# Loading one piece of the output weight in two transfers, 108 and 20 partitions, in a decode block on one core

## The chip, the cores and the metric

The kernel runs on one core of one Trainium2 chip. The metric is the device time of one launch in microseconds (us). The kernel before takes 1302.96 us, the median of three runs (1302.74 to 1303.16).

## The reference

The block normalises its input and adds three things: the input, an attention block over a cache of 4096 keys, and a small MLP. Everything is float32.

```python
x = A_x                                   # [4, 1, 512]
xn = layernorm(x)
q = (xn @ A_wq).reshape(4, 1, 32, 128)    # 32 heads of 128
scores = einsum("bhqd,bhkd->bhqk", q, A_k_cache) * 128**-0.5    # caches: [4, 32, 4096, 128]
o = einsum("bhqk,bhkd->bhqd", softmax(scores), A_v_cache)
att = o.reshape(4, 1, 4096) @ A_wo        # A_wo: [4096, 512]
# mlp: sequence length is 1, so the token shift leaves only zeros and x1 = xn
mlp = xn + gelu(layernorm(xn) @ B_w3) @ B_w4
return x + att + mlp                      # [4, 1, 512]
```

The two caches are 268 MB each. All the weights together are about 24 MB.

## The kernel before, in words

The 128 pairs of batch and head are handled in 32 steps of four heads (`NJ = 32`, `G = 4`). A step reads 8 MB of keys into one of two buffers (`ks[0]`, `ks[1]`) and 8 MB of values into `vs`. VectorE (DVE) multiplies the keys by the query (L329) and sums (L330), in two halves. ScalarE (ACT) takes the exponential (L348). TensorE (PE) multiplies the probabilities with the values (L382).

All these loads are issued by SyncE (SP), one after the other in the order of the code, on one DMA queue (q1 in the profile). SP waits for a semaphore before most issues: `summed` says that DVE has used half a key buffer, `done` says that a step's values have been used.

After the last step comes the tail, where this change lies. The output weight `wo` is laid out as 128 partitions of 32 rows (`wo_r`, partition p holds rows 32p to 32p + 31, each of 512 floats or 2 KB), and it goes into the key buffer of the last step. SP issues it as soon as DVE has read that buffer for the last time (`SUMMED[LAST]`), in seven pieces that become smaller:

```python
wo_cuts = ((0, 16), (16, 24), (24, 28), (28, 30), (30, WC - 1))
```

These are rows per partition: the five pieces hold 16, 8, 4, 2 and 1 rows per partition, and two more pieces hold the halves of row 31 (L292). Each piece has its own semaphore (`wo0` to `wo6`), and each of its partitions is one contiguous run in memory: 32, 16, 8, 4, 2, 1 and 1 KB. "The piece with two rows per partition" is the fourth, `wo3`: 128 runs of 4 KB, 512 KB in all.

PE waits for the pieces one by one and multiplies the attention output `X` with each row. Rows 0 to 23 go into `y` (L419). Rows 24 to 30 go into `total` through the helper `blocks4` (L151), and so does the sum over `y`, which ACT has copied to `os` first (L425). The two halves of row 31 come last (L434). Then DVE (L436) and ACT (L437) copy the result out of PSUM, and two small DMAs store it (L441).

Of the kernel before, what the change touches and what calls it, by code (L numbers as in the profile page):

```python
# [44 lines left out]
P = 128  # L45
# [4 lines left out]
PE, DVE, ACT = mybir.EngineType.PE, mybir.EngineType.DVE, mybir.EngineType.Activation  # L50
# [38 lines left out]
def decode_block(ctx: ExitStack, tc: tile.TileContext, x, k, v, wq, wo, w3, w4, out):  # L89
    nc = tc.nc  # L90
# [10 lines left out]
    FT = F // 4  # L101
    WC = H * DH // P
    LAST = NJ - 1

    def sb(name, *shape):
        return nc.alloc_sbuf_tensor(name, [P, *shape], F32).ap()
# [37 lines left out]
    def rows(flat, j):  # L144
        n = G * S * DH
        return flat[j * n:(j + 1) * n].rearrange("(p n) -> p n", p=P)

    def blocks4(start, stop, w, m, src):

        for t in range(4):  # L150
            i = nc.tensor.matmul(total[32 * t:32 * t + m, :], w, src[:, P * t:P * t + P], start=start, stop=stop)  # L151
        return i

    do = Steps(nc)
    wo_sems = [nc.alloc_semaphore(f"wo{n}") for n in range(7)]
    sems = {n: nc.alloc_semaphore(n) for n in (
        "x", "w3", "wq", "k0", "k1", "landed", "last", "w4", "go", "pv", "copied", "poz",
        "half0", "half1", "nm", "dve", "summed", "expd", "done", "bye", "out")}
    wo_sb = ks[LAST % 2].rearrange("p (c n) -> p c n", c=WC)
    wo_cuts = ((0, 16), (16, 24), (24, 28), (28, 30), (30, WC - 1))  # L160
# [3 lines left out]
    def load(o, i, sem, by, *after, queue="SP"):  # L164
        return do(queue, lambda e: e.dma_start(o, i), *after, done=(sems[sem], 16, by))
# [22 lines left out]
        out=ident, in_=ident, compare_op=ALU.not_equal, fill=1.0, base=0, pattern=[[-1, P]],  # L188
# [64 lines left out]
    for c in range(NC):  # L253
        for t in range(4):
# [23 lines left out]
             for i, n in enumerate((0, HALF))]  # L278
    for j in range(LAST - 1):
        if j > 0:  # L280
            load(ks[j % 2], rows(kf, j + 2), f"k{j % 2}", None, SUMMED[j])
        load(vs, rows(vf, j + 1), "landed", None, DONE[j])
    last_in = load(ks[(LAST - 1) % 2], rows(vf, LAST), "last", 16, SUMMED[LAST - 1])
    w4_in = load(w4_sb, w4.rearrange("(p m) n -> p m n", m=NF), "w4", 16, DONE[LAST - 1])
    do.wait("SP", [SUMMED[LAST]])
    wo_r = wo.rearrange("(p c) n -> p c n", c=WC)
    for (c0, c1), sem in zip(wo_cuts, wo_sems):
        nc.sync.dma_start(wo_sb[:, c0:c1], wo_r[:, c0:c1]).then_inc(sem, 16)
    half = D // 2
    for n, sem in enumerate(wo_sems[-2:]):  # L290
        n *= half
# [10 lines left out]
    nc.gpsimd.sem_inc(sems["k0"], 16)  # L302
    d = do("POOL", lambda e: e.memset(g4, 0.0), DONE[LAST - 1])
    g4_ok = do("POOL", lambda e: e.tensor_copy(g4[:, :, 0:B], gT[:, 0:4, :]), d, gT_ok)
# [4 lines left out]
    with nc.Fori(0, NJ // 2, engines=OrderedEngineSet([DVE]), head_slot={DVE: 192}) as j:  # L309
        e, n = nc.vector, 0  # L310
# [92 lines left out]
    for m in range(NF):  # L403
        t, g, n = (m, g4[:, m, :], 32) if m < 4 else (m % 4, gT[:, m, :], B)
# [7 lines left out]
    ys = os.rearrange("p m d -> p (m d)")  # L412
    do.wait("PE", [X_ok])
    for (c0, c1), sem in zip(wo_cuts, wo_sems):
        do.wait("PE", [(sem, 16)])
        for c in range(c0, c1):
            if c < 24:
                t = (c + 2) % 4
                i = nc.tensor.matmul(y[32 * t:32 * t + B, :], X[:, c, :], wo_sb[:, c], start=False, stop=(c >= 20))  # L419
            else:  # L420
                i = blocks4(False, False, X[:, c, :], B, wo_sb[:, c])
        d = do("PE", lambda e: i)

        if c1 == 24:
            ys_ok = do("ACT", lambda e: e.copy(ys, y), d)  # L425
        elif c1 == 28:
            do.wait("PE", [ys_ok])
            blocks4(False, False, sel, 32, ys)
# [15 lines left out]
    nc.sync.sem_inc(sems["bye"], 1)  # L444
    nc.scalar.sem_inc(sems["bye"], 1)
    nc.gpsimd.wait_ge(sems["bye"], 2)
    nc.clear_and_free_semaphores([*do.sem.values(), *wo_sems, *(h for n, h in sems.items() if n != "out")])
    do.wait("SP", [stored])
    nc.sync.sem_inc(sems["out"], -32)

# [27 lines left out]
```

## Time and profile before

| what | value |
|---|---|
| median of three runs | 1302.96 us |
| the profiled execution, from its first to its last instruction (its span) | 1301.5 us |
| what the median has beyond that span | 1.46 us |
| busy share of DVE, PE, ACT | 89%, 28%, 7% |
| DMA: bytes read, mean rate over the span | 561 MB, 431 GB/s |
| issue of the first piece of `wo` | 1267.41 us |
| first matmul with `wo` | 1289.46 us |
| first matmuls with the two halves of row 31 (their weight loads) | 1299.12 and 1299.44 us |

No other time is recorded for the profiled execution than its span; the runs were made without a profile. Differences within the trace are used as they stand, and a sum is made against the span and carried over to the median. In the windows, "DMA share" is the busy share of the core's 16 DMA engines, so a share times 16 is the number of engines at work. "PEld" is a weight load of PE, which shows when PE got past a wait. Times in the timeline are from the start of the span.

### The profile page before, as it was taken

Reading aid. Unit: us, or ns where it says so; the run is one execution under the profiler, and the core shown is the slowest. Engines: PE = TensorE matmul, PEld = TensorE weight load, DVE = VectorE, ACT = ScalarE, POOL = GpSimd, SP = SyncE. Lnnn points to the kernel's source line nnn. Section 1 sums busy time; section 2 is a strip of 40 time slices with the busy share of each in tenths; the row PEclk is TensorE's granted clock in tenths of the full one; section 3 lists DMA queues with packets and bytes.
Section 4 is the critical chain, followed back from the end, with each engine's and each line's share of the span. In section 5 each row is a group of like instructions: output and inputs, shape, how many; then the busy total and the mean of one; then the engine's idle time right before and its main releaser. Section 6 shows DMA issues by size and latency. Waiting matters only on the chain. (4 is left out here: it accounts for less than half of the span.)

```text
span 1301.5 us, 6687 instructions
## 1 busy us (share of the span) xinstructions
PE 368.7 (28%) x2652; PEld 132.8 (10%) x2652; DVE 1164.4 (89%) x323; ACT 93.5 (7%) x332; POOL 2.5 (0%) x14
## 2 busy tenths in 40 slices
PE   4121332321233321133331133332123332123337
PEld 2000111100011100011110011110011110001112
DVE  2599999999999999999999999999999999999990
ACT  0100000000000000000000000000000000000001
POOL 0000000000000000000000000000000000000000
PEclk9555666655666655666655566665566665566668
DMA  9999999999999999999999999999999999999998
GB/s 404 448 421 449 423 441 427 435 435 425 443 423 447 423 447 421 441 429 431 439 421 447 423 447 423 445 423 437 433 425 445 421 447 423 447 423 443 425 426 367
DMA packets 10830, 561.08 MB, mean 431 GB/s; under 512 B 1212, under 2 KB 1476, under 8 KB 1736
## 3 DMA queue, kind: packets, MB, share of 16 engines
q1 hardware_dynamic: 10808, 561.00, 99.7%
q8 instruction: 3, 0.05, 0.0%
q14 instruction: 3, 0.02, 0.0%
q10 hardware_dynamic: 16, 0.01, 0.0%
HBM read 561.00 MB, written 0.01 MB: 431 GB/s over the span
## 5 line engine op out<-in xcount | busy, mean ns | idle before, releaser
L329 DVE TENSOR_TENSOR ks<-ks,qb 128x8192 f32<-128x8192 f32 x64 | 556.3, 8692 | 63.7 <-DVEq L297 58.7
L330 DVE TENSOR_REDUCE sc<-ks 128x64 f32<-128x8192 f32 x64 | 555.9, 8686 | 2.2
L382 PE MATMUL pv<-vs,pw 128*32 128x512 f32 x1984 | 286.9, 743 | 874.9 <-PEq L297 874.9
L382 PEld LDWEIGHTS pv<-vs,pw 128*32 128x32 f32 x1984 | 79.2, 133 | 1057.9 <-issue 1057.9
L353 ACT COPY os<-pv 128x512 f32<-128x512 f32 x32 | 18.7, 585 | 827.8 <-ACTq L297 827.8
L348 ACT ACTIVATE pw<-sc,small 32x128 f32<-32x128 f32 x128 | 50.9, 398 | 278.1 <-ACTq L297 276.9
L387 PE MATMUL poz<-sel,os 128*128 128x4 f32 x256 | 32.8, 252 | 28.0 <-PEq L297 28.0
L387 PEld LDWEIGHTS poz<-sel,os 128*128 128x128 f32 x256 | 31.0, 191 | 56.1 <-issue 56.1
L348 ACT ACTIVATION_READ_ACCUMULATOR pw<-sc,small 32x1 f32 x128 | 23.5, 184 | 0.0
L436 DVE COPY os<-total 4x128 f32<-4x128 f32 x2 | 0.6, 282 | 16.2 <-PE total L434 16.2
L335 DVE TENSOR_REDUCE small<-sc 128x1 f32<-128x128 f32 x32 | 9.2, 286 | 4.7
L363 DVE RECIPROCAL rz<-oz 128x96 f32<-128x96 f32 (+1 forms) x2 | 1.1, 552 | 12.6 <-ACT oz L355 12.5
L389 PE MATMUL poz<-rs,ones 128*128 128x4 f32 x64 | 11.7, 253 | 0.0
L245 DVE STREAM_TRANSPOSE vs<-pw 128x1024 f32<-128x1024 f32 x1 | 1.2, 1245 | 10.9 <-ACT pw L244 10.9
L321 DVE STREAM_TRANSPOSE qb<-qg 128x128 f32<-128x128 f32 x32 | 10.0, 312 | 1.1
L202 DVE TENSOR_REDUCE lns<-vs 4x1 f32<-4x512 f32 x1 | 0.7, 674 | 11.3 <-DMA vs<-in_A_x_dram 11.3
L320 DVE COPY qg<-qT 128x4 f32 x32 | 5.4, 170 | 4.9 <-issue 4.9
L389 PEld LDWEIGHTS poz<-rs,ones 128*128 128x128 f32 x64 | 9.7, 192 | 0.0
L215 PE MATMUL pt<-vs,pw 4*128 4x4 f32 x16 | 4.0, 372 | 18.1 <-DVE pw L209 18.1
L419 PE MATMUL y<-ks,X 128*4 128x512 f32 x48 | 8.0, 835 | 3.5 <-DMA ks<-in_A_wo_dram 3.5
L355 ACT COPY oz<-poz 128x8 f32 x32 | 5.3, 165 | 50.8 <-ACTq L297 50.8
L382 PE MATMUL pv<-ks,pw 128*32 128x512 f32 x64 | 8.5, 692 | 0.0
(75 smaller groups left out, 74.8 us busy)
## 6 DMA issues: line engine op xcount, KB each, us to landing
ks<-in_A_k_cache_dram SPq DMA_DIRECT2D x2, 4096.0 KB, 26.9
vs<-in_B_w_dram SPq DMA_DIRECT2D x2, 3584.0 KB, 23.1
ks<-in_A_wo_dram SPq DMA_DIRECT2D x1, 4096.0 KB, 21.9
ks<-in_A_wo_dram SPq DMA_DIRECT2D x1, 2048.0 KB, 26.5
ks<-in_A_wo_dram SPq DMA_DIRECT2D x1, 1024.0 KB, 28.6
ks<-in_A_wo_dram SPq DMA_DIRECT2D x1, 512.0 KB, 29.4
ks<-in_A_k_cache_dram SPq DMA_DIRECT2D x31, 42.2
vs<-in_A_v_cache_dram SPq DMA_DIRECT2D x31, 26.8
```

Source lines behind the costliest of these rows:

```text
L320: step(e.tensor_copy(qg, pairs[:, s, bass.ds(j, 1)].rearrange("p o n -> p (o n)")))
L321: step(e.transpose(qb.rearrange("p (n m) -> p n m", m=HP), qg.unsqueeze(2).to_broadcast([P, DH // HP, HP])))
L329: step(e.tensor_tensor(out=kt, in0=kt, in1=qb.unsqueeze(1).to_broadcast([P, w, DH]), op=ALU.mult))
L330: step(e.reduce_sum(sc[s][:, c:c + w], kt, axis=AX.X))
L335: step(e.reduce_max(rm, sc[s], axis=AX.X))
L348: i = nc.scalar.activation(pw[hp, :, 4 * h:4 * h + 4], sc[s][hp, :].rearrange("p (g w) -> p g w", w=4), AF.Exp, bias=small[hp, s, 1:2], sc ...
L353: nc.scalar.copy(os, pv.rearrange("p (m d) -> p m d", m=4)).then_inc(sems["copied"], 1)
L355: nc.scalar.copy(ozs[:, s, :, bass.ds(j, 1)].rearrange("p n o h -> p n (o h)"), poz[:, 0:2 * G].rearrange("p (n h) -> p n h", n=2)).then_i ...
L382: i = nc.tensor.matmul(pv[32 * t:32 * t + 32, :], pw[:, g, :], vt[:, 4 * g:4 * g + 4, :], start=(g < 4), stop=(g >= NG - 4))
L387: nc.tensor.matmul(poz[:, 0:G], os[:, m, :], sel.rearrange("p (h m) -> p m h", m=4)[:, m, 0:G], start=(m == 0), stop=(m == 3))
L389: nc.tensor.matmul(poz[:, G:2 * G], ones.to_broadcast([P, P]), rs, start=True, stop=True).then_inc(sems["poz"], 1)
L419: i = nc.tensor.matmul(y[32 * t:32 * t + B, :], X[:, c, :], wo_sb[:, c], start=False, stop=(c >= 20))
```

## The change

The fourth piece, `wo3`, is no longer one transfer. Its partitions 0 to 107 are loaded where the whole piece was, between `wo2` and `wo4`. Its partitions 108 to 127 are loaded by a transfer of their own, which SP issues directly behind the first piece `wo0`, with its own semaphore `low`. PE waits for both semaphores before it uses rows 28 and 29.

```diff
+    FEW, TOP = 3, 108
...
+    low_sem = nc.alloc_semaphore("low")
...
-    for (c0, c1), sem in zip(wo_cuts, wo_sems):
-        nc.sync.dma_start(wo_sb[:, c0:c1], wo_r[:, c0:c1]).then_inc(sem, 16)
+    for n, ((c0, c1), sem) in enumerate(zip(wo_cuts, wo_sems)):
+        top = TOP if n == FEW else P
+        nc.sync.dma_start(wo_sb[:top, c0:c1], wo_r[:top, c0:c1]).then_inc(sem, 16)
+        if n == 0:
+            c0, c1 = wo_cuts[FEW]
+            nc.sync.dma_start(wo_sb[TOP:, c0:c1], wo_r[TOP:, c0:c1]).then_inc(low_sem, 16)
...
     for (c0, c1), sem in zip(wo_cuts, wo_sems):
-        do.wait("PE", [(sem, 16)])
+        do.wait("PE", [(sem, 16), *([(low_sem, 16)] if (c0, c1) == wo_cuts[FEW] else [])])
```

The order in which SP issues its last transfers, before. A row gives the line, the tile and its source, and partitions by elements per partition (1024 elements are the two rows of `wo3`):

```order
L165 DMA vs<-in_B_w_dram 128x7168 [waits done]
L288 DMA ks<-in_A_wo_dram 128x8192 [waits summed]
L288 DMA ks<-in_A_wo_dram 128x4096
L288 DMA ks<-in_A_wo_dram 128x2048
L288 DMA ks<-in_A_wo_dram 128x1024
L288 DMA ks<-in_A_wo_dram 128x512
L292 DMA ks<-in_A_wo_dram 128x256 x2
L441 DMA out_dram<-os 4x256 [waits nACT,nDVE]
```

The same place on SP now:

```order
L167 DMA vs<-in_B_w_dram 128x7168 [waits done]
L291 DMA ks<-in_A_wo_dram 128x8192 [waits summed]
L294 DMA ks<-in_A_wo_dram 20x1024
L291 DMA ks<-in_A_wo_dram 128x4096
L291 DMA ks<-in_A_wo_dram 128x2048
L291 DMA ks<-in_A_wo_dram 108x1024
L291 DMA ks<-in_A_wo_dram 128x512
L298 DMA ks<-in_A_wo_dram 128x256 x2
L447 DMA out_dram<-os 4x256 [waits nACT,nDVE]
```

The transfer of 20 partitions is new in second place; the fourth piece keeps its place with 108 partitions, and six issues move back by one.

On PE, the end of the program before, from the last wait for a four-row piece on, with the semaphores that each group waits for:

```order
L151 MATMUL total<-ks,X 4x128 [waits wo2]
L151 MATMUL total<-ks,X 4x128 x15
L151 MATMUL total<-os,sel 32x128 [waits nACT]
L151 MATMUL total<-os,sel 32x128 x3
L151 MATMUL total<-ks,X 4x128 [waits wo3]
L151 MATMUL total<-ks,X 4x128 x7
L151 MATMUL total<-ks,X 4x128 [waits wo4]
L151 MATMUL total<-ks,X 4x128 x3
L434 MATMUL total<-ks,X 4x128 [waits wo5]
L434 MATMUL total<-ks,X 4x128
L434 MATMUL total<-ks,X 4x128 [waits wo6]
L434 MATMUL total<-ks,X 4x128
```

And now:

```order
L152 MATMUL total<-ks,X 4x128 [waits wo2]
L152 MATMUL total<-ks,X 4x128 x15
L152 MATMUL total<-os,sel 32x128 [waits nACT]
L152 MATMUL total<-os,sel 32x128 x3
L152 MATMUL total<-ks,X 4x128 [waits low,wo3]
L152 MATMUL total<-ks,X 4x128 x7
L152 MATMUL total<-ks,X 4x128 [waits wo4]
L152 MATMUL total<-ks,X 4x128 x3
L440 MATMUL total<-ks,X 4x128 [waits wo5]
L440 MATMUL total<-ks,X 4x128
L440 MATMUL total<-ks,X 4x128 [waits wo6]
L440 MATMUL total<-ks,X 4x128
```

No matmul moves; the group for rows 28 and 29 has one wait more. DVE, ACT and GpSimd keep their instructions in their order.

More of the change, by code (lines that the diff above doesn't have):

```diff
@@ L446, in decode_block @@
     nc.gpsimd.wait_ge(sems["bye"], 2)
-    nc.clear_and_free_semaphores([*do.sem.values(), *wo_sems, *(h for n, h in sems.items() if n != "out")])
+    nc.clear_and_free_semaphores([*do.sem.values(), *wo_sems, low_sem, *(h for n, h in sems.items() if n != "out")])
     do.wait("SP", [stored])
```

## The prediction

> **What bounds the kernel now.** I read the page's DMA queues first, then the table of windows, then the timeline of the tail. The page says that one queue keeps the engines busy for all of the span:
>
> ```profile
> q1 hardware_dynamic: 10808, 561.00, 99.7%
> ```
>
> So the time up to the tail is the time of 561 MB, and the change touches neither those bytes nor their order until the first piece of `wo`. What it can change is the tail. Its windows (columns: stretch in us, its length, then busy time and count of PE, PEld, DVE, ACT, POOL, then PE clock, DMA share, GB/s):
>
> ```profile
> 50.00:1250.00 1200.00, 314.57 (x2220) 112.32 (x2220) 1129.95 (x282) 83.23 (x308) 0.00 (x0) 0.61 1.00 434
> ...
> 1297.00:1297.50 0.50, 0.50 (x19) 0.21 (x10) 0.00 (x0) 0.00 (x0) 0.00 (x0) 1.00 0.71 248
> 1297.50:1298.00 0.50, 0.50 (x28) 0.46 (x20) 0.00 (x0) 0.48 (x1) 0.00 (x0) 1.00 0.30 111
> 1298.00:1298.50 0.50, 0.50 (x24) 0.37 (x20) 0.00 (x0) 0.11 (x1) 0.00 (x0) 1.00 0.21 74
> 1298.50:1299.00 0.50, 0.50 (x28) 0.39 (x18) 0.00 (x0) 0.00 (x0) 0.00 (x0) 1.00 0.14 47
> ```
>
> Two things stand here. At a share of 1.00 the 16 engines move 434 GB/s, so one engine moves 27.1 GB/s and a run of 4 KB costs it 4096 / 27.1 = 0.151 us. And the engines do not finish together: 0.71 x 16 is 11.4 engines at work, then 4.8, 3.4 and 2.2. About eleven are done by 1297.5, while two or three go on for almost 1.5 us. If three engines last to the end, 2.2 of 3 times 0.5 us puts them at 1298.87. The other 0.4 engine of the window before is then a fourth that ends near 1298.2, and a fifth ends near 1297.9.
>
> Why some are late can be seen in the same queue table, taken for three short stretches (32.8 to 33.2, 1273 to 1274.6 and 1293 to 1293.5; columns: packets, MB, share of 16 engines' time):
>
> ```profile
> q8 instruction: 1, 0.02, 15.6%
> ...
> q8 instruction: 1, 0.02, 4.3%
> q14 instruction: 1, 0.01, 1.2%
> ...
> q8 instruction: 1, 0.02, 13.6%
> ```
>
> Instructions are fetched by the same engines. The three q8 packets held one engine for 0.156 x 0.4 x 16 = 1.0 us, 0.043 x 1.6 x 16 = 1.1 us and 0.136 x 0.5 x 16 = 1.1 us. That is the size of the lag of the late ones. Since all engines otherwise run at one pace without a pause, an engine that is once behind stays behind.
>
> Now what the late engines cost. The timeline of the tail (weight loads, then matmuls, then ACT; the brackets hold the idle time before and what ended it):
>
> ```profile
> 1295.13 0.10 PEld L419 LDWEIGHTS y<-ks,X 128*4 128x4 f32 x4 [0.44 <-issue]
> ...
> 1296.88 0.10 PEld L151 LDWEIGHTS total<-ks,X 128*4 128x4 f32 x4 [0.37 <-DMA ks<-in_A_wo_dram]
> ...
> 1298.16 0.16 PEld L151 LDWEIGHTS total<-os,sel 128*32 128x32 f32 x8
> 1298.30 0.65 PEld L151 LDWEIGHTS total<-ks,X 128*4 128x4 f32 x24
> 1299.12 0.10 PEld L434 LDWEIGHTS total<-ks,X 128*4 128x4 f32 x4 [0.17 <-DMA ks<-in_A_wo_dram]
> 1299.44 0.10 PEld L434 LDWEIGHTS total<-ks,X 128*4 128x4 f32 x4 [0.22 <-DMA ks<-in_A_wo_dram]
> ...
> 1289.46 7.99 PE L419 MATMUL y<-ks,X 128*4 128x512 f32 x48 [3.48 <-DMA ks<-in_A_wo_dram]
> 1297.27 1.05 PE L151 MATMUL total<-ks,X 128*4 128x128 f32 x32
> ...
> 1297.52 0.58 ACT L425 COPY os<-y 128x512 f32<-128x512 f32 x1 [11.13 <-PE y L419]
> ```
>
> PE starts on the first piece at 1289.46 and has no gap until the two halves of row 31. There it waits for a DMA twice, 0.17 and 0.22 us. These 0.39 us are all that an earlier end of the late engines can bring. The rest of PE's tail hangs on its own matmuls and on ACT's copy. In the other direction nothing covers: a later end of the last engine goes straight into the 0.22 us wait and the time.
>
> **The change, part by part.**
>
> How the rows fall on the engines. The packets show how a transfer is split. First a stretch of 4.5 us with the load of `x` (4 partitions, the q10 row), then the last 39.5 us:
>
> ```profile
> DMA packets 40, 2.11 MB, mean 468 GB/s; under 512 B 4, under 2 KB 4, under 8 KB 8
> ...
> q10 hardware_dynamic: 8, 0.01, 0.5%
> ...
> DMA packets 1223, 14.47 MB, mean 366 GB/s; under 512 B 152, under 2 KB 416, under 8 KB 672
> ```
>
> The load of 4 rows has 8 packets: 4 rows and 4 tiny ones that close it. In the last stretch there are 152 tiny ones: 8 for the two stores of 4 rows, and 144 = 9 x 16 for the nine transfers of 128 rows that end in it. So each engine that takes part closes its share once; 128 rows go to 16 engines, 8 rows each, and 4 rows to 4 engines, one each. Both are equal shares. If shares must be equal, 108 rows can go to no more than 12 engines (9 rows each) and 20 rows to no more than 10 (2 each), as 16 to 13 do not divide 108 and 16 to 11 do not divide 20. No row shows either of these sizes, so this is taken from the two that are shown.
>
> With those shares, four engines lose all 8 of their rows of `wo3`: 8 x 0.151 = 1.21 us less. Twelve get one row more, 0.15 us, and ten of the sixteen get two rows from the new transfer, 0.30 us. An engine that has both carries 3 rows more, 0.45 us. The trace does not number the engines, so it doesn't say which kind the late ones are.
>
> [...]
>
> The end of the last engine. The bounds are -0.39 us (both waits gone) and +0.45 us (a late engine carries three rows more). If the three late ones are among the four that lose rows, they end at 1298.87 - 1.21 = 1297.7, and the fourth becomes the last: 1298.2 + 0.45 = 1298.65, that is 0.22 us earlier than now. I take -0.22 us, inside the -0.39 us. It is a guess a little over even: the late engines, three by the windows, are no more than the four that are relieved, while a single one left out turns the sign.
>
> The order of issue. SP spends 0.50 us on each issue:
>
> ```profile
> 1267.41 2.50 SPq L288 DMA_DIRECT2D ks<-in_A_wo_dram  x5
> 1269.96 0.90 SPq L292 DMA_DIRECT2D ks<-in_A_wo_dram  x2
> ...
> ks<-in_A_wo_dram SPq DMA_DIRECT2D x1, 4096.0 KB, 21.9
> ks<-in_A_wo_dram SPq DMA_DIRECT2D x1, 2048.0 KB, 26.5
> ks<-in_A_wo_dram SPq DMA_DIRECT2D x1, 1024.0 KB, 28.6
> ```
>
> One more issue in second place moves the other six back by 0.50 us. The DMA queue is over 20 us behind the issues (21.9 us from the issue of the first piece to its landing), so this costs nothing. Without that backlog it would be 0.50 us. SP has nothing after them but the store, 29 us later.
>
> Two rows more ahead of the second and third piece: 0.30 us on ten engines. The second piece lands about 1267.9 + 26.5 = 1294.4, and PE takes row 16 (the 33rd weight load of L419) at 1295.13. 0.7 us cover the 0.30. The third piece is awaited until 1296.88, but the matmuls behind that weight load start at 1297.27, when PE is free. 0.39 us cover 0.30; if they didn't, ACT's copy up to 1298.10 is late next, and it hangs on `y` alone. I take 0, at most 0.1 us.
>
> PE's added wait for `low`. These rows land right behind the first piece, near 1289.5, and PE asks at 1298.30. Queued behind it are the matmuls of rows 28 to 31. The nearest row is the wait for `wo3` in the same place, where the weight loads of 1298.16 and 1298.30 follow each other without a gap. I take 0, at most 0.1 us for one more instruction.
>
> The sum is -0.22 us on the span of 1301.5, and on the median 1302.96 - 0.22 = 1302.7 us. The median has 1.46 us that lie outside the span, which the change doesn't touch.
>
> **The rivals.** Differences under 0.2% (2.6 us) can't be told from no change in this kernel; all but one of these cases lie within.
>
> *A late engine is loaded, not relieved.* One of the three late ones is among the ten that carry three rows more: the last half of row 31 comes 0.45 us later, 1303.4 us. For it: twelve engines get more and only four less, and one late engine among them decides. Against it: only that all three share the cause of their lag, and may share their place. [...]
>
> *The change does not do what it says.* The transfers of 108 and 20 rows are spread as evenly as 128 were, 8 rows per engine in sum, or a late engine gains and loses about as much. Then only the order of rows differs, and the time stays 1303.0 us. The 4-row transfer with one row on each of 4 engines neither excludes nor supports it.
>
> *The split falls on far fewer engines.* If the number must divide 16 as well, as both sizes that the trace shows (16 and 4) do, 108 rows go to 4 engines, 27 each, and 20 to 4, 5 each. Four engines would carry 32 rows where they carried 8: 24 x 0.151 = 3.6 us more. They end at 1297.5 + 3.6 = 1301.1 if they are early ones, 2.2 us after the last one now, and at 1302.5 if a late one is among them, 3.6 us after. That gives 1305.2 to 1306.6 us, slower by over 0.2% if the worst of the four ends now after 1297.9. Against it: only the packets of two sizes speak for it.
>
> **How the numbers follow.** Forecast, late engines relieved: 0.48, at 1302.7. A late engine loaded: 0.36, at 1303.4. No difference in the shares: 0.09, at 1303.0. Few engines: 0.05, at 1305.2 to 1306.6, and over the bound in more than half of that, 0.03. The remaining 0.02 are for something unseen, a fetch of instructions that falls elsewhere for example, half of it on each side. Within 0.2% is thus 0.95, slower 0.04, faster 0.01. The range goes from 1302.96 - 0.39 = 1302.6, less the runs' own spread of 0.4 us, to 1303.4 and the same spread: 1302.2 to 1303.8.
>
> **What the profile after would show.** If the forecast holds, the windows after 1297.5 have a smaller share at the end, about 0.02 to 0.08 in 1298.5 to 1299.0, the waits of 0.17 and 0.22 us before the halves of row 31 shrink to under 0.2 us together, and the weight load of the second half comes near 1299.2. The number of tiny packets in the tail tells the split: 12 + 10 closing packets for the two transfers, so 6 more than before, against 16 more for an even split and 8 fewer for four engines each. If a late engine is loaded, the wait before the second half grows by up to 0.45 us and the share in the last window stays or rises. A landing of the four-row piece after 1297.3, or a gap before the weight loads of 1298.30, would show that the 20 rows ahead were not covered. I am wrong if the time moves by more than 0.5 us to either side.

## The result and the profile after

The changed kernel takes 1305.78 us (median of 12 runs, 1304.71 to 1306.76). The kernel before takes 1302.80 us (12 runs, 1302.62 to 1303.22). The ratio is 1.0022, with a 95% interval of 1.0014 to 1.0029: slower by 3.0 us, and outside my range of 1302.2 to 1303.8. The profiled execution took 1304.87 us, with a span of 1303.5 us against 1301.5 before, so its trace shows 2.0 of the 3.0 us.

Up to the tail nothing differs: both kernels run at a DMA share of 1.00 and 434 GB/s from 50 to 1250 us. These are the windows after (the last two columns are DMA share and GB/s; a packet counts whole in the window in which it starts, so the share of a short window can pass 1, and the next one is then too low):

```profile
50.00:1250.00 1200.00, 315.14 (x2220) 111.94 (x2220) 1130.01 (x282) 83.21 (x308) 0.00 (x0) 0.61 1.00 434
...
1288.00:1289.00 1.00, 0.00 (x0) 0.00 (x0) 0.00 (x0) 0.00 (x0) 0.00 (x0) 0.91 0.67 229
...
1295.00:1296.00 1.00, 1.00 (x12) 0.24 (x8) 0.00 (x0) 0.00 (x0) 0.00 (x0) 0.68 0.93 322
1296.00:1297.00 1.00, 1.00 (x16) 0.21 (x12) 0.00 (x0) 0.00 (x0) 0.00 (x0) 1.00 1.11 252
1297.00:1298.00 1.00, 1.00 (x12) 0.10 (x4) 0.00 (x0) 0.00 (x0) 0.00 (x0) 1.00 0.91 225
1298.00:1299.00 1.00, 0.67 (x20) 0.43 (x20) 0.00 (x0) 0.58 (x1) 0.00 (x0) 1.00 0.97 240
```

The same stretches of before, as far as the prediction did not show them:

```profile
1288.00:1289.00 1.00, 0.00 (x0) 0.00 (x0) 0.00 (x0) 0.00 (x0) 0.00 (x0) 0.52 0.96 410
...
1295.00:1296.00 1.00, 1.00 (x16) 0.21 (x12) 0.00 (x0) 0.00 (x0) 0.00 (x0) 1.00 1.01 410
1296.00:1297.00 1.00, 1.00 (x16) 0.29 (x12) 0.00 (x0) 0.00 (x0) 0.00 (x0) 1.00 1.00 371
```

The rate falls in two places: about 1288, when the 20 rows run (over 1287 to 1289 together it is 277 GB/s at a share of 0.97, against 410 at 0.96 before), and from 1295 on, when the 108 rows run. A "row" of a transfer is here and below the run that it loads into one partition. From 1296 to 1299 the engines are busy all the time (1.11, 0.91, 0.97) and move 225 to 252 GB/s. A busy share near 1 with about half the rate means that each packet takes longer: in this trace 0.256 us on average for a 4 KB row of the 108, against 0.161 for a row of that size before. It does not mean that engines stand still or have more to carry.

PE and the weight loads after:

```profile
1290.25 7.99 PE L425 MATMUL y<-ks,X 128*4 128x512 f32 x48 [3.89 <-DMA ks<-in_A_wo_dram]
...
1298.56 0.77 PEld L152 LDWEIGHTS total<-ks,X 128*4 128x4 f32 x32 [1.26 <-DMA ks<-in_A_wo_dram]
...
1300.34 0.55 PEld L152 LDWEIGHTS total<-ks,X 128*4 128x4 f32 x24 [0.77 <-DMA ks<-in_A_wo_dram]
1301.11 0.10 PEld L440 LDWEIGHTS total<-ks,X 128*4 128x4 f32 x4 [0.22 <-DMA ks<-in_A_wo_dram]
1301.43 0.10 PEld L440 LDWEIGHTS total<-ks,X 128*4 128x4 f32 x4 [0.23 <-DMA ks<-in_A_wo_dram]
```

The first piece lets PE start at 1290.25 instead of 1289.46, 0.79 us later. The third piece comes at 1298.56 instead of 1296.88. Rows 28 and 29 wait until 1300.34 (1298.30 before, without a wait), and the last half of row 31 until 1301.43 instead of 1299.44. These 1.99 us are the longer span.

The DMA table of the last 41.5 us, with the landing times of the first three pieces:

```profile
DMA packets 1227, 14.34 MB, mean 345 GB/s; under 512 B 158, under 2 KB 422, under 8 KB 678
...
ks<-in_A_wo_dram SPq DMA_DIRECT2D x1, 4096.0 KB, 22.7
...
ks<-in_A_wo_dram SPq DMA_DIRECT2D x1, 2048.0 KB, 26.8
ks<-in_A_wo_dram SPq DMA_DIRECT2D x1, 1024.0 KB, 29.9
```

There are 158 tiny packets where there were 152. Six more is what the prediction gave for 12 + 10 engines.

### The profile page after: what moved, and what is told of

Its sections match the earlier page's. It is cut to its first block, busy times and chain, and to the rows that moved or that the text cites. A ratio compares the mean times of both kernels' runs of the same rounds, so it can differ in the third digit from the quotient of the medians.

```text
span 1303.5 us, 6689 instructions
## 1 busy us (share of the span) xinstructions
PE 369.1 (28%) x2652; PEld 132.2 (10%) x2652; DVE 1164.5 (89%) x323; ACT 93.5 (7%) x332; POOL 2.5 (0%) x14
```

## The experiments

I tested these theories; the expectations use their letters.

- D, destination: which partitions of SBUF a transfer writes decides how long its rows take. The expectations speak of inlets, ways into SBUF that engines share at some sets of partitions; no trace here shows an inlet, or which partitions share one.
- N, number and shares: 12 and 10 engines with unequal shares cost the time.
- O: one more transfer, or its place behind the first piece, costs by itself.
- H: the way in which the source is read costs the time.

All edits are against the changed kernel's loop, unless said otherwise.

| run | us, median (range) | before, same chip | ratio, 95% interval |
|---|---|---|---|
| split by rows | 1302.96 (1302.66 to 1303.23) | 1302.78 | 1.0001 (0.9991 to 1.0011) |
| 20 extra rows, high | 1303.67 (1303.53 to 1303.97) | 1302.78 | 1.0007 (0.9997 to 1.0017) |
| 20 extra rows, spread | 1303.34 (1303.10 to 1303.54) | 1302.78 | 1.0005 (0.9995 to 1.0014) |
| 20 extra rows, high, packed source | 1303.80 (1303.53 to 1304.06) | 1302.88 | 1.0007 (0.9998 to 1.0017) |
| cut 112 and 16 | 1304.89 (1304.49 to 1305.60) | 1302.78 | 1.0018 (1.0008 to 1.0028) |
| 108 and 20 both in place | 1304.84 (1304.25 to 1305.74) | 1302.88 | 1.0017 (1.0007 to 1.0026) |
| 108 alone | 1304.39 (1303.47 to 1305.28) | 1302.88 | 1.0012 (1.0003 to 1.0022) |
| 108 alone, packed source | 1304.51 (1303.52 to 1304.92) | 1302.75 | 1.0013 (1.0004 to 1.0023) |
| first piece in halves | 1316.03 (1315.14 to 1317.73) | 1302.88 | 1.0099 (1.0082 to 1.0116) |
| first piece, 32 to 95 only | 1298.09 (1297.80 to 1300.16) | 1302.76 | 0.9967 (0.9957 to 0.9977) |
| first piece, 0 to 63 only | 1306.63 (1305.11 to 1308.01) | 1302.76 | 1.0029 (1.0019 to 1.0038) |
| fourth piece, 32 to 95 only | 1302.33 (1302.24 to 1302.84) | 1302.75 | 0.9997 (0.9988 to 1.0007) |
| fourth piece, 0 to 63 only | 1304.01 (1303.65 to 1305.39) | 1302.75 | 1.0011 (1.0001 to 1.0020) |
| 12 engines loaded | 1303.71 (1303.33 to 1304.72) | 1302.76 | 1.0008 (0.9998 to 1.0017) |
| 10 engines loaded | 1303.76 (1303.20 to 1304.59) | 1302.76 | 1.0008 (0.9999 to 1.0018) |

**The same order, cut by rows.**

```diff
+        if n == FEW:
+            c0 += 1
-        nc.sync.dma_start(wo_sb[:top, c0:c1], wo_r[:top, c0:c1]).then_inc(sem, 16)
+        nc.sync.dma_start(wo_sb[:, c0:c1], wo_r[:, c0:c1]).then_inc(sem, 16)
         if n == 0:
             c0, c1 = wo_cuts[FEW]
-            nc.sync.dma_start(wo_sb[TOP:, c0:c1], wo_r[TOP:, c0:c1]).then_inc(low_sem, 16)
+            nc.sync.dma_start(wo_sb[:, c0:c0 + 1], wo_r[:, c0:c0 + 1]).then_inc(low_sem, 16)
```

> The fourth piece is again loaded in two transfers, one of them directly behind the first piece, but cut by rows: row 28 of all 128 partitions early, row 29 of all 128 in its place. Theory D (destination: too many engines write to few partitions' inlets at once, since 108 and 20 partitions are not spread as 128 are): no loss, 1302.8 us +-0.4. Theory N (number of engines: 12 and 10 instead of 16 carry unequal shares, which alone costs the time): no loss either, 1302.8. Theory O (one more transfer, or 2 KB per partition in front of the second piece, costs by itself): the first piece lands about 0.8 us later as it did after the change, 1303.6 us or more.

The first piece lands after 21.9 us, as before:

```profile
ks<-in_A_wo_dram SPq DMA_DIRECT2D x1, 4096.0 KB, 21.9
```

It took 1302.96 us, no change that can be told. One transfer more, one issue more on SP, one wait more on PE and even three times as many bytes in front of the second piece (256 KB instead of 80) cost nothing that shows. Theory O falls.

**The 20 rows alone, and where they land.** The fourth piece stays whole; 20 extra rows go into unused space.

```diff
+    free = vs[:, 8192:9216].rearrange("p (c n) -> p c n", c=2)
-        top = TOP if n == FEW else P
-        nc.sync.dma_start(wo_sb[:top, c0:c1], wo_r[:top, c0:c1]).then_inc(sem, 16)
+        nc.sync.dma_start(wo_sb[:, c0:c1], wo_r[:, c0:c1]).then_inc(sem, 16)
...
-            nc.sync.dma_start(wo_sb[TOP:, c0:c1], wo_r[TOP:, c0:c1]).then_inc(low_sem, 16)
+            nc.sync.dma_start(free[TOP:], wo_r[TOP:, c0:c1]).then_inc(low_sem, 16)        # high
+            nc.sync.dma_start(free[0:120:6], wo_r[TOP:, c0:c1]).then_inc(low_sem, 16)     # spread
+            nc.sync.dma_start(free[TOP:], wo.rearrange("(p c) n -> p c n", c=2)[:P - TOP]).then_inc(low_sem, 16)  # packed
```

The high partitions:

> The fourth piece is whole and in its place; behind the first piece the 20 partitions 108 to 127 are loaded once more, into unused space of the value buffer at the same partitions 108 to 127 (80 KB extra). Theory D: the first piece lands 0.8 us later than in the kernel before, and the end comes 0.8 to 1.1 us later, 1303.6 to 1303.9 us. Theory N: only the two rows on ten engines, 0.30 us, 1303.1 us. Theory H (the source: 20 runs of 4 KB at 64 KB pitch slow the memory down): as D.

The spread partitions:

> The same extra transfer of 20 rows from the same source, but it lands at partitions 0, 6, 12 and so on to 114. Number of rows, engines and source are the same as with the 20 high partitions. Theory D: no more than its bytes, 0.1 to 0.3 us, 1302.9 to 1303.1 us, and the first piece lands within 0.3 us of the kernel before. Theory N: the same as with the high partitions. Theory H: the same as with the high partitions, 1303.6 to 1303.9 us.

The packed source:

> The whole fourth piece in place and 20 extra rows into partitions 108 to 127 of unused space, as in the run with the extra rows at high partitions, but read from 80 KB that lie in one piece instead of at 64 KB pitch (the values loaded are not used). Theory D: the same as with the pitch, first piece 0.8 to 1.2 us later, 1303.6 us +-0.3. Theory H (the source's pitch): as with spread partitions or better, 1302.9 to 1303.3 us.

The window in which the rows run, and the landing of the first piece (21.9 us before), with the high partitions:

```profile
1288.00:1289.00 1.00, 1.00 (x6) 0.27 (x2) 0.00 (x0) 0.00 (x0) 0.00 (x0) 1.00 0.86 279
...
ks<-in_A_wo_dram SPq DMA_DIRECT2D x1, 4096.0 KB, 22.9
```

And with the spread ones:

```profile
1288.00:1289.00 1.00, 0.00 (x0) 0.00 (x0) 0.00 (x0) 0.00 (x0) 0.00 (x0) 1.00 0.89 356
...
ks<-in_A_wo_dram SPq DMA_DIRECT2D x1, 4096.0 KB, 22.0
```

Same rows, same source, same number of engines (162 tiny packets in the tail of both): at neighbouring partitions the first piece lands 1.0 us later than before, at spread ones 0.1 us. With the packed source it was 22.8, as with the pitch. So for the 20 rows the destination makes the delay of the first piece, and H falls. In time the difference is smaller, 1303.67 against 1303.34 us. The spread rows still cost 0.56 us, more than the 0.30 us of their bytes that I allowed. The intervals of all three against before include no change. Only the direct comparison tells high from spread: the lowest of the one (1303.53) and the highest of the other (1303.54) just touch.

**Equal shares on 16 engines.**

```diff
-    FEW, TOP = 3, 108
+    FEW, TOP = 3, 112
```

> The change with the cut at 112 instead of 108: 112 partitions in place, 16 behind the first piece. Both numbers are multiples of 16, so by equal shares all 16 engines carry 7 and 1 rows, 8 as before the change. Theory N: no loss, 1302.8 us +-0.4. Theory D: 16 engines write to 16 neighbouring partitions, and 7 rows per engine do not fall as 8 do; slower than before by 1.5 to 3.5 us, 1304.3 to 1306.3 us.

```profile
1296.00:1297.00 1.00, 1.00 (x16) 0.20 (x11) 0.00 (x0) 0.00 (x0) 0.00 (x0) 1.00 0.96 213
1297.00:1298.00 1.00, 1.00 (x12) 0.10 (x4) 0.00 (x0) 0.00 (x0) 0.00 (x0) 1.00 1.00 224
...
DMA packets 1237, 14.34 MB, mean 341 GB/s; under 512 B 168, under 2 KB 432, under 8 KB 688
```

Sixteen more tiny packets (168 against 152) show that both transfers run on all 16 engines, so by equal shares each engine carries 8 rows as before the change. The rate falls to 213 GB/s all the same, and the time is 2.1 us longer. Theory N falls as the cause: unequal shares aren't needed for the loss.

**The 108 rows, with and without the others.** In the first run the 20 rows follow the 108 in place; in the second they are left out; in the third the 108 rows come from a packed source as well. Where the 20 are left out, PE does not wait for them either.

```diff
+        if n == FEW:                                # both in place
-        if n == 0:
-            c0, c1 = wo_cuts[FEW]
             nc.sync.dma_start(wo_sb[TOP:, c0:c1], wo_r[TOP:, c0:c1]).then_inc(low_sem, 16)    # left out in the other two
...
+    packed = wo.rearrange("(p c) n -> p c n", c=2)
+        i = packed[:TOP] if n == FEW else wo_r[:, c0:c1]    # third run: the source i
```

> The change with the 20 rows issued directly behind the 108, in the place of the fourth piece, so nothing is put behind the first piece. Theory D (destination: the partitions of such a transfer fall on the engines and on the memory's inlets otherwise than 128 do, and the inlets become the limit): the first and second piece land as in the kernel before, the loss comes from the fourth piece on, 1304.5 to 1306.5 us. If the loss came from the early place of the 20 rows: 1302.8 us +-0.4.

> The fourth piece with 108 partitions in its place, and the other 20 partitions not loaded at all (80 KB left out, so two rows of 20 partitions hold old values). No transfer behind the first piece. Theory D: the fourth piece alone slows the last pieces, 1304 to 1305.5 us. Theory N (unequal shares): at most one row more on twelve engines, 0.15 us, and four are relieved, 1302.5 to 1303.1 us.

> The fourth piece with 108 partitions alone, as in the run that left out the other 20, but read from 432 KB that lie in one piece instead of runs at 64 KB pitch (the values of these rows are then others, and 20 partitions are not loaded). Theory D (crowding at the inlets): as with the pitch, 1304.4 us +-0.5. Theory H (the way in which twelve engines with nine rows each walk through the source): the loss of 1.5 us goes, 1302.5 to 1303.1 us.

The 108 alone, then the 108 alone from the packed source:

```profile
1295.00:1296.00 1.00, 0.96 (x12) 0.03 (x4) 0.00 (x0) 0.00 (x0) 0.00 (x0) 1.00 0.95 218
1296.00:1297.00 1.00, 0.00 (x0) 0.00 (x0) 0.00 (x0) 0.58 (x1) 0.00 (x0) 1.00 0.99 242
1297.00:1298.00 1.00, 0.00 (x0) 0.00 (x0) 0.00 (x0) 0.00 (x0) 0.00 (x0) 1.00 0.95 225
```

```profile
1295.00:1296.00 1.00, 1.00 (x16) 0.22 (x12) 0.00 (x0) 0.00 (x0) 0.00 (x0) 1.00 1.05 248
1296.00:1297.00 1.00, 1.00 (x12) 0.10 (x4) 0.00 (x0) 0.00 (x0) 0.00 (x0) 1.00 0.91 221
1297.00:1298.00 1.00, 0.25 (x6) 0.01 (x3) 0.00 (x0) 0.58 (x1) 0.00 (x0) 1.00 0.97 235
```

The source makes no difference here either (1304.39 and 1304.51 us). With nothing put ahead of it, the third piece, whose four rows per partition are issued before the 108, comes late all the same. This is PE's first load from it with the 108 alone (1296.88 in the kernel before):

```profile
1298.24 0.77 PEld L152 LDWEIGHTS total<-ks,X 128*4 128x4 f32 x32 [3.21 <-DMA ks<-in_A_wo_dram]
```

The medians add up in steps: the 108 alone cost 1304.39 - 1302.88 = 1.5 us; the 20 in place behind them another 0.45 (1304.84); and putting the 20 behind the first piece instead of in place another 0.94 (1305.78, with the two medians of before 0.08 apart).

**Which 64 partitions.** To see the destination alone, I took transfers of 64 partitions, which run on 16 engines with 4 rows each whichever 64 they are (the tail has 152 tiny packets with either set, as before). The changed kernel's extra transfer is gone, and of one piece only 64 partitions are loaded; in the run with halves both are.

```diff
-        top = TOP if n == FEW else P
-        nc.sync.dma_start(wo_sb[:top, c0:c1], wo_r[:top, c0:c1]).then_inc(sem, 16)
+        lo, hi = (32, 96) if n == 0 else (0, P)          # or (0, 64); or n == FEW
+        nc.sync.dma_start(wo_sb[lo:hi, c0:c1], wo_r[lo:hi, c0:c1]).then_inc(sem, 16)
```

> The kernel before, with the first piece (4 MB) loaded as two transfers of partitions 0 to 63 and 64 to 127, one behind the other. Both numbers are multiples of 16, so all 16 engines carry 4 + 4 rows, 8 as before. Theory D: if 64 neighbouring partitions reach half of the inlets, each transfer runs at half the rate, the 4 MB take 19.3 us instead of 9.7, and the time is up to 9.7 us longer, 1310 to 1313 us. Theory N: no loss, 1302.8 us +-0.5.

> Of the first piece only partitions 32 to 95 are loaded (2 MB; the other 64 partitions of 16 rows are left out and hold old values). [...] Theory D with inlets: full rate, 2 MB less are 4.8 us less, 1297.5 to 1298.7 us. A theory by which any transfer of other than 128 partitions is slow: 1302 to 1305 us, as with partitions 0 to 63.

> The same with partitions 0 to 63 (2 MB, the other 64 partitions left out). Theory D with inlets: half the rate or less, so the saved 4.8 us are lost again, 1302.8 to 1304.6 us. Theory N (number of engines and shares): 16 engines with 4 rows each, as with 32 to 95, 1298 us.

The first piece in halves:

```profile
1292.00:1294.00 2.00, 0.00 (x0) 0.00 (x0) 0.00 (x0) 0.00 (x0) 0.00 (x0) 1.00 1.04 213
1294.00:1296.00 2.00, 0.00 (x0) 0.00 (x0) 0.00 (x0) 0.00 (x0) 0.00 (x0) 0.60 1.20 246
1296.00:1298.00 2.00, 0.00 (x0) 0.00 (x0) 0.00 (x0) 0.00 (x0) 0.00 (x0) 0.50 0.64 131
```

Partitions 32 to 95 only:

```profile
1282.00:1284.00 2.00, 2.00 (x22) 0.98 (x25) 0.83 (x3) 0.17 (x1) 0.00 (x0) 1.00 0.91 385
1284.00:1286.00 2.00, 2.00 (x19) 0.29 (x8) 0.00 (x0) 0.00 (x0) 0.00 (x0) 1.00 1.00 426
```

Partitions 0 to 63 only:

```profile
1282.00:1284.00 2.00, 2.00 (x21) 0.94 (x25) 0.84 (x3) 0.17 (x1) 0.00 (x0) 1.00 1.28 262
1284.00:1286.00 2.00, 2.00 (x16) 0.29 (x8) 0.00 (x0) 0.00 (x0) 0.00 (x0) 1.00 1.12 229
```

2 MB on 16 engines with equal shares run at 426 GB/s into partitions 32 to 95 and at 229 into 0 to 63, and the times are 8.5 us apart. Half of 434 is 217. This is the clearest sign for theory D: it isn't the count of partitions, it is which ones. The full rate for 32 to 95 and half of it for 0 to 63, from which D's two forecasts start, came from the inlets, which no run shows; what the runs show is the two rates. The two runs also read different rows of `wo`, 64 neighbouring ones each at the same pitch; no run changes the source of this pair alone. That the source doesn't matter is taken from the packed sources above, and from the 20 rows, where one source gave two results. I missed upward twice: the halves cost 13.2 us (four runs) where I gave at most 9.7, and 0 to 63 took 1306.63 us where I gave 1304.6. The 131 above is a window beside one of 246; from 1284 to 1302 as a whole the halves run at 205 GB/s. Most of what goes beyond 9.7 us is in the table of row durations below: a row takes 2.1 times as long, and the piece behind the halves is slowed too.

The same pair at the fourth piece's own place, loaded to partitions 32 to 95 alone and then to 0 to 63 alone (256 KB each; the other 256 KB of the piece are left out):

> Of the fourth piece only partitions 32 to 95 in its place (256 KB; the other 64 partitions are left out). [...] Theory D: nothing lost, and 4 rows of 0.15 us less on each engine, as far as PE's other work lets it through, 1302.2 to 1302.7 us. If any transfer of other than 128 partitions is slow at this place: 1303.5 us or more.

> [...] Theory D: the 0.6 us saved are lost and more, since engines ahead stand in the way of the late ones, 1303.0 to 1304.5 us; slower than with 32 to 95 by 0.6 us at least. Theory N (number of engines and shares): the same as with 32 to 95.

Partitions 32 to 95, then 0 to 63:

```profile
1295.00:1296.00 1.00, 1.00 (x12) 0.11 (x4) 0.00 (x0) 0.00 (x0) 0.00 (x0) 1.00 1.02 395
1296.00:1297.00 1.00, 0.38 (x16) 0.24 (x16) 0.00 (x0) 0.58 (x1) 0.00 (x0) 1.00 0.73 256
```

```profile
1295.00:1296.00 1.00, 1.00 (x14) 0.10 (x4) 0.00 (x0) 0.00 (x0) 0.00 (x0) 1.00 0.98 143
1296.00:1297.00 1.00, 0.29 (x4) 0.00 (x0) 0.00 (x0) 0.59 (x1) 0.00 (x0) 1.00 0.94 208
1297.00:1298.00 1.00, 0.00 (x0) 0.00 (x0) 0.00 (x0) 0.00 (x0) 0.00 (x0) 1.00 1.03 216
```

1302.33 against 1304.01 us, with equal engines and shares. 256 KB, which take 0.6 us at the full rate, hold the rate down for three microseconds at partitions 0 to 63. That is the same picture as with the 108 and the 112 rows. (The profiled execution with 0 to 63 is the slowest of its ten, 1305.39 us, and from 1299 on it has PE at a granted clock of 0.50 to 0.65 as well; the comparison rests on the medians and on the windows before that.)

**Would the late engines have been relieved?** The fourth piece is whole; behind the first piece 12 or 10 extra rows of 32 KB go into unused space, at partitions 32, 36 and so on to 76 or to 68. A row of that size took 1.217 us in the kernel before.

```diff
+    free = vs[:, 8192:].rearrange("p (c n) -> p c n", c=16)
...
+            nc.sync.dma_start(free[32:80:4], wo_r[32:80:4, c0:c1]).then_inc(low_sem, 16)    # or 32:72:4
```

> The whole fourth piece in place. [...] If a transfer of 12 partitions runs on 12 engines, each carries 1.2 us more and four none, which is what the change was to do to the late engines, without the crowding. If the three late engines are among the four: they are the last no longer by much, +0.3 to 0.6 us, 1303.1 to 1303.4 us. If one of the late ones is among the twelve: +1.2 us, 1304.0 us +-0.2.

> As with 12 extra rows, but 10 rows at partitions 32 to 68, so ten engines carry 1.2 us more and six none. If no late engine is among the ten: +0.3 to 0.6 us, 1303.1 to 1303.4 us. If one is: 1304.0 us +-0.2. With the run of 12 this says whether the late engines would have been relieved.

With 12 rows, in the window in which they run, and the tiny packets of the tail:

```profile
1288.00:1289.00 1.00, 0.00 (x0) 0.00 (x0) 0.00 (x0) 0.00 (x0) 0.00 (x0) 0.78 0.89 377
...
DMA packets 1246, 14.80 MB, mean 361 GB/s; under 512 B 164, under 2 KB 428, under 8 KB 684
```

Twelve more tiny packets (164) mean twelve engines, and 377 GB/s is near the 410 of before: this transfer on twelve engines isn't slow. No packet of 32 KB took longer than 1.23 us in this tail, the same as before. On the late engines the pair does not decide. Both took 0.95 to 1.0 us more, between the 0.3 to 0.6 for one answer and the 1.2 for the other. Which engines are late stays open.

## Why the prediction was wrong

The split over the engines was right: six more tiny packets, so 12 and 10 engines. The two costs taken at 0 for SP's issue and PE's wait held as well; the kernel cut by rows has both and shows no loss.

The step that failed is the price of a row. I took 4 KB as 0.151 us of one engine, from the rate of 434 GB/s over 16 engines, and I took the change to leave the price of all other rows alone. The profile of before had no large transfer other than of 128 partitions from which I could have seen that this does not hold for other shapes. The traces keep the duration of every packet, and its size names the piece (32 KB is a row of the first, 4 KB one of the fourth). These are the mean durations in us in the tail:

| trace | first piece, 32 KB | second, 16 KB | fourth, 4 KB | fifth, 2 KB |
|---|---|---|---|---|
| before | 1.217 | 0.615 | 0.161 | 0.086 |
| after | 1.236 | 0.681 | 0.256 | 0.129 |
| 108 alone | 1.217 | 0.615 | 0.256 | 0.136 |
| 20 extra rows, high | 1.239 | 0.684 | 0.161 | 0.085 |
| 12 engines loaded | 1.217 | 0.614 | 0.162 | 0.085 |
| first piece in halves | 2.583 | 0.852 | 0.161 | 0.084 |

A row of the 108 takes 0.256 us instead of 0.161. The 20 rows, at 0.205 us each, are not the slow ones: with them four rows of the first piece take up to 2.02 us instead of 1.22, and rows of the second piece are slower too, although both pieces have all 128 partitions. The rows of all pieces of `wo` together take 35 us more after than before, that is 2.2 us for each of 16 engines, and the span of that trace is 1.99 us longer: the durations account for the loss. In the same way the halves come to 12.8 us, beside a span that is 14.9 us longer (13.2 us in the medians).

So the 0.30 us for two rows and the 0.45 us for three were too small, and my bounds from them were no bounds: the first piece, which I did not expect to move, landed 0.8 us later, and the 108 rows, priced at 0.15 us more on twelve engines, cost 1.5 us.

The covers went with it, but the sign that I named for them was a wrong one. I wanted to read from a landing after 1297.3 that the 20 rows are not covered. PE got the third piece at 1298.56, and with the 108 alone, where no row is put ahead, at 1298.24.

The gain of 0.22 us, from relieved engines that end 1.21 us earlier, never showed. The two waits before the halves of row 31 are 0.22 and 0.23 us, no smaller than before, and they only come 1.99 us later. Whether the late engines are among the four without a share is not settled, and at this price it does not matter.

One rival came out near the measured time, few engines at 1305.2 to 1306.6 us, but by another mechanism; that its number is close is luck. It asked for eight tiny packets fewer; there are six more. The chance of 0.04 on slower by over 0.2% rested on that rival for the most part, and it was too small: I asked how many engines take part and how much each carries, and not where they write.

Why a row of the 108 takes 0.256 us the traces do not show: they name neither the engine of a packet nor its way into SBUF. What is shown: the number of engines and unequal shares (1304.89 us with equal shares on 16), one more transfer (1302.96 us) and the pitch of the source (1304.39 us with it, 1304.51 without) are not what makes the loss, and for the 20 rows it follows the partitions that are written, with all else held (the first piece 1.0 us late or 0.1). For the sets of 64 the rows that are read change too, and the 108 rows were written to one set of partitions only. The runs are also further apart after the change (2.05 us between the lowest and the highest, 0.60 before).

## What to carry to other kernels

Keep loads into SBUF at all 128 partitions, and cut them along the other dimension when a part has to come earlier: the cut by rows cost nothing that shows, the cut by partitions 3 us, and a 4 MB load cut into two halves of 64 partitions 13 us. When a DMA's busy share stays near 1 and its rate falls, look at which partitions its packets go to before counting engines or bytes. No version here beats the kernel before: the two with a lower median leave part of the weight out.

## What was not expected of the hardware

A small transfer slowed much more than itself: 80 KB into 20 neighbouring partitions made a 4 MB piece, issued ahead of them, land 1.0 us later: five of its 128 rows took up to 1.82 us instead of 1.22. What holds those five rows up, no trace shows. And 64 partitions are not like 64 others: 426 GB/s into 32 to 95, 229 GB/s into 0 to 63.
